# Attention in units of both heads, the causal mask added by TensorE, one maximum per unit, and a new written order up to MLP 1's ninth step

## The chip, the cores and the metric

The kernel runs on 1 core of one Trainium2 chip. The metric is the device time of one execution in microseconds (us). The engines are named as in the profile: PE is TensorE (PEld its weight loads), DVE VectorE, ACT ScalarE, POOL GpSimd, SP SyncE. Each engine works through its own instructions in the order in which the program writes them.

## The reference

The function computes causal attention with a learned decay, then two MLPs on its output. Cut to what matters:

```python
scores = scale * np.matmul(q, k.transpose(0, 1, 3, 2))        # 2 batches x 8 heads, 576 x 64
cum = np.cumsum(np.maximum(s, 0.0), axis=-1)
bias = -(cum[:, :, :, None] - cum[:, :, None, :])
scores = np.where(causal, -1000000000.0, scores + np.minimum(bias, 0.0))
scores = scores - np.max(scores, axis=-1, keepdims=True)
attn = np.exp(scores)
attn = attn / (np.sum(attn, axis=-1, keepdims=True) + 1e-09)
x = np.matmul(attn, v)                                        # -> 1152 tokens x 512
xn = x / np.sqrt(np.mean(x * x, axis=-1, keepdims=True) + 1e-06) * rms_g
h1 = (silu(xn @ w_gate) * (xn @ w_val)) @ w_out               # d_ff 1536
h = h1 @ w_in                                                 # d_ff 2048
out = (h * np.tanh(log1p(exp(h)))) @ w_out2
```

## The kernel before

**Attention.** The 16 heads go as 8 pairs of heads (NP). For a pair the scores are products of 64 rows of queries with 64 rows of keys, each split in a high and a low part so that one product of 128 rows (L359) and one of 68 rows (L360; four of these carry the bias of the decay) give them exactly enough. A head's 576 rows are tiles 0 to 3 of 128 rows and a last one of 64. `qk_unit` writes five units per pair: u0 and u1 hold tiles 0 and 1 of head 0 and head 1, in one PSUM bank each; u2 and u3 hold tiles 2 and 3 of head 0 and head 1, two banks each; u4 holds the last 64 rows of both heads, in two banks (L366, L367). Four single banks (`psS`) take them in turn. For each piece of a unit one custom VectorE instruction (`maxes`, L384) adds the causal mask from SBUF, multiplies by -0.125, writes the sum back and leaves the minimum in `sbias`; ScalarE takes the exponential with that bias and leaves the row's sum (`exps`, L391). TensorE transposes the probabilities (`pt_transposes`, L407), ScalarE, for u3 VectorE, copies them out (`pt_evac`), and TensorE multiplies with V in two parts (`av_op`, L445): part 0 for tiles 0 and 1, part 1 for the rest. The result is copied (`xt_evac`), transposed back (`x_transposes`, L456, tile xq) and multiplied by the reciprocal of the sums (`recips`, L462 to L465, and `x_norm`, L475).

For each pair POOL issues the transfers of keys and queries (`load_k`, `load_q`, `load_cum`), and computes three of the four low parts (`k_lo` L125, `q_lo` L131); VectorE computes the fourth. While attention runs, weights are already loaded and converted (`w_load`, `w_a` on ScalarE, `w_b` on VectorE at L276 and L278, `w_c` on ScalarE and, as long as attention runs, POOL at L296); `w_tick` does one such step.

**MLP 1.** Tokens go in blocks of 384. A step (b, f) multiplies block b by gate and value chunk f (`gate_val`, L549, 24 matmuls into two banks, gv), `silu_a` makes mbuf, `silu_b` splits it in the two parts of hhl, and `y_acc` (L583, 12 matmuls) adds the step to four banks. Batch 1's normalisation falls into the first steps: squares (`xn_sq`), twelve small VectorE operations for the reciprocal root (`rsqrt_ops`, L489 to L499), scaling, four times five transposes (`xn_mm`, L517) and the copies xh and xl (`xn_evac`, L523 and L524).

**What sets the order.** Everything is written out by hand: `at(t, f, ...)` collects calls with a time t in units, they are sorted by t and called in that order; attention uses this, and MLP 1's steps from k = 1 on are a loop behind it. No scheduler moves anything.

Of the kernel before, what the change touches and what calls it, by code (L numbers as in the profile page):

```python
# [12 lines left out]
ALU = mybir.AluOpType  # L13

# [29 lines left out]
def tile_kernel(ctx: ExitStack, tc: tile.TileContext, kq, qq, v, s, w1, w2, rms_g, out):  # L44
# [7 lines left out]
    psS = [ctx.enter_context(ExitStack())]  # L52
    psS.append(psS[0].enter_context(tc.tile_pool(name="psS", bufs=4, space=bass.MemoryType.PSUM)))
# [17 lines left out]
    raw = [[rawt[2 * i + h][:, 0:S] for h in range(2)] for i in range(2)]  # L71

# [4 lines left out]
    for i in range(2):  # L77
# [9 lines left out]
        PTB.append([w[:, 1280 * h:1280 * h + 1280].rearrange("p (c n) -> p c n", c=4) for h in range(2)])  # L87
        PTA.append([w[:, 2560:2944], xat[i][:, 2560:2944]])
        PTC.append([w[0:64, 2944 + 64 * h:3008 + 64 * h] for h in range(2)])
# [63 lines left out]
    nc.gpsimd.memset(mask16, 0.0)  # L153
    nc.gpsimd.affine_select(out=mask16[:, 384:512], in_=mask16[:, 384:512], pattern=[[-1, 128]], compare_op=ALU.is_ge,
                            fill=-8e9, base=0, channel_multiplier=1)
# [28 lines left out]
    def gates(h, x, pools):  # L184
        co = slice(64 + 288 * x, 352 + 288 * x)
        t = []
        for y, (pool, tag) in enumerate(pools):
            t.append(pool.tile([128, 512], F32, tag=tag, name="gates"))
# [6 lines left out]
    pT, pX, pS = (psT, "T"), (psX, "X"), (psS[1], "S")  # L195
# [12 lines left out]
    k_lo(0, 1, nc.gpsimd)  # L208
    nc.gpsimd.memset(mask16j, 0.0)
    for h in range(2):  # L210
        m = mask16j[64 * h:64 * h + 64, 224:288]
        nc.gpsimd.affine_select(out=m, in_=m, pattern=[[-1, 64]], compare_op=ALU.is_ge, fill=-8e9, base=0,
                                channel_multiplier=1)
# [112 lines left out]
    NU = 5 * NP  # L326


    def unit_tiles(u):
        return (0, 1) if u < 2 else (2, 3)  # L330

    s_tile = {}
    pos = [(2, 0, 1, 3, 4).index(i) if i < 5 else i for i in range(NU)]

    def s_views(i):
        u, t = i % 5, s_tile[i]
        if u == 4:
# [12 lines left out]
    def qk_unit(i):  # L350
        p, u = divmod(i, 5)
        z = p % 2
        s_tile[i] = [psS[1].tile([128, 512], F32, tag="S", name="sc") for _ in range(1 if u < 2 else 2)]
        if u < 4:
            hh = u % 2
            for o, n in zip(s_views(i), unit_tiles(u)):
                qs = slice(704 * hh + 128 * n, 704 * hh + 128 * n + 128)
                ks = slice(S * hh, S * hh + 128 * (n + 1))
                nc.tensor.matmul(o, QA[z][:, qs], KA[z][:, ks], start=(n != 1), stop=False)  # L359
                nc.tensor.matmul(o, QB[z][0:68, qs], KB[z][0:68, ks], start=False, stop=(n != 0))  # L360
        else:
            for n, o in enumerate(s_views(i)):
                for hh in range(2):
                    qs = slice(512 + 64 * hh, 640 + 64 * hh)
                    ks = slice(S * hh + 288 * n, S * hh + 288 * n + 288)
                    nc.tensor.matmul(o, QB[z][0:68, qs], KB[z][0:68, ks], start=(hh == 0), stop=False)  # L366
                    nc.tensor.matmul(o, QA[z][:, qs], KA[z][:, ks], start=False, stop=(hh == 1))  # L367

    def ring_col(i):
        return 2 * (pos[i] % 4)  # L370

    def sum_cols(i):

        p, u = divmod(i, 5)
        c = 12 * (p % 2)
        return [c + 8, c + 9] if u == 4 else [c + 2 * n + u % 2 for n in unit_tiles(u)]

    def maxes(i):

        for x, sv in enumerate(s_views(i)):  # L380
            u, c = i % 5, ring_col(i) + x
            m = (mask16[:, 0:288], mask16j)[x] if u == 4 else mask16[:, 512 - sv.shape[-1]:512]
            first = 3e38 if u < 4 or x == 0 else sbias[:, c - 1:c]
            nc.vector.tensor_tensor_reduce(out=sv, in0=sv, in1=m, scale=-0.125, scalar=first, op0=ALU.add, op1=ALU.min,  # L384
                                           accum_out=sbias[:, c:c + 1])

    def exps(i):
        c = ring_col(i)
        for x, (sv, pv, sc) in enumerate(zip(s_views(i), p_views(i), sum_cols(i))):
            x = 1 if i % 5 == 4 else x  # L390
            nc.scalar.activation(out=pv, in_=sv, func=ACTF.Exp, bias=sbias[:, c + x:c + x + 1], scale=-1.0,  # L391
# [9 lines left out]
    def pt_transposes(i):  # L401
        u = i % 5
        t_tile[i] = []
        for a, e, rows in pt_parts(u):
            t = psT.tile([128, 512], F32, tag="T", name="tp")
            for o in range(a, e, 128):
                nc.tensor.transpose(t[0:rows, o - a:o - a + 128], P[pos[i] % 2][:, o:min(e, o + 128)], ident)  # L407
            t_tile[i].append(t)

    def pt_evac(i):  # L410
        p, u = divmod(i, 5)
        z, t = p % 2, t_tile.pop(i)
        if u < 2:
            cp = [(PTA[z][u], t[0][:, 0:384])]
        elif u < 4:
            cp = [(PTB[z][u - 2][:, 0:n, 128 * y:128 * y + 128], t[y][:, 0:128 * n].rearrange("p (c n) -> p c n", c=n))
                  for y, n in enumerate((3, 4))]
        else:
            cp = [(PTB[z][h][:, :, 256:320], t[0].rearrange("p (c n) -> p c n", c=4)[:, :, 64 * h:64 * h + 64])
                  for h in range(2)]  # L420
            cp += [(PTC[z][h], t[1][0:64, 64 * h:64 * h + 64]) for h in range(2)]
        for dst, src in cp:
            if u == 3:
                nc.vector.tensor_copy(out=dst, in_=src)
            else:
                nc.scalar.copy(out=dst, in_=src)
# [3 lines left out]
    def av_op(p, part, c):  # L430
# [5 lines left out]
        for h in range(2):  # L436
# [463 lines left out]
```

## Time and profile before

| | us |
|---|---|
| median of 3 runs | 557.2 (555.62 to 557.57) |
| the profiled execution's own time | 557.82 |
| its span in the trace | 556.0 |
| PE busy | 535.5 (96%) |
| DVE busy | 284.8 (51%) |
| ACT busy | 255.8 (46%) |
| POOL busy | 66.8 (12%) |
| mean granted TensorE clock | 0.991 of full speed |

The span runs from the first to the last instruction of the trace; the execution's own time has 1.8 us around it. Busy time of one engine overlaps that of the others.

### The profile page before, as it was taken

The numbers are of one execution on the slowest core, as the hardware profiler recorded it, in microseconds if no ns is written. First come the engines' busy times: TensorE is split into PE (matmuls) and PEld (weight loads), VectorE is DVE, ScalarE is ACT, GpSimd is POOL, SyncE is SP. The second block draws the span as 40 slices with busy tenths as digits, with TensorE's granted clock in tenths as the row PEclk, the third lists the DMA queues.
The fourth block names the chain that finished last, engine by engine and source line by source line (L and its number), as shares of the span: only waits on it lengthen the run. The fifth ranks groups of instructions, "written<-read, shape, count | busy, mean of one in ns | idle before, by whom it ended". The sixth has DMA issues, their size and how long they took to land.

```text
span 556.0 us, 7854 instructions
## 1 busy us (share of the span) xinstructions
PE 535.5 (96%) x3008; PEld 484.5 (87%) x3008; DVE 284.8 (51%) x626; ACT 255.8 (46%) x581; POOL 66.8 (12%) x77
## 2 busy tenths in 40 slices
PE   5989999999699999999999999999999999999997
PEld 4666766789589999999999999999899899899895
DVE  7769999868736733677422256488711011011011
ACT  6767998858726522455321144455512211221211
POOL 6557856300000000000000000000000000000000
PEclk9989999999889999999999999999999999999999
DMA  9889894256714521554400004025201000010001
GB/s 239 224 228 230 241 239 121 77 192 228 223 39 146 159 75 34 168 177 152 151 2 1 0 4 144 6 78 184 79 0 58 1 0 1 0 58 1 1 0 58
DMA packets 18782, 55.91 MB, mean 101 GB/s; under 512 B 2348, under 2 KB 2604, under 8 KB 18716
## 3 DMA queue, kind: packets, MB, share of 16 engines
q1 hardware_dynamic: 13520, 42.04, 23.5%
q0 software_dynamic: 3712, 9.70, 8.5%
q10 hardware_dynamic: 1512, 3.66, 2.3%
q8 instruction: 24, 0.39, 0.3%
q14 instruction: 14, 0.11, 0.1%
HBM read 52.73 MB, written 2.66 MB: 100 GB/s over the span
## 4 chain that ended last, share of the span: by engine, by line
PE 84%; DVE 6%; DMA 3%; issue 2%; ACT 2%; POOL 1%; POOLq 0%; ACTq 0%; DVEq 0%
PE gv L549 25%; PE gv L618 18%; PE o L659 18%; PE y L583 12%; PE xa L445 4%; PE tp L407 3%; DMA w<-in_kq_dram 1%; DMA w<-in_qq_dram 1%; PE sc L360 1%; PE sc L359 1%; DVE sc L384 1%; PE xq L456 1%; DVE w L296 1%; DMA scr<-cC 1%; POOL w L131 1%
## 5 line engine op out<-in xcount | busy, mean ns | idle before, releaser
L549 PE MATMUL gv<-xh,wt 128*128 128x384 f32 x384 | 102.0, 336 | 1.2 <-DVE xl L524 1.2
L646 DVE TENSOR_TENSOR glb<-u,glb 128x768 fp32r<-128x768 f32 (+1 forms) x25 | 23.1, 925 | 115.8 <-ACT glb L645 115.7
L549 PEld LDWEIGHTS gv<-xh,wt 128*128 128x128 f32 x384 | 69.8, 188 | 1.5 <-issue 1.3
L557 ACT ACTIVATE mbuf<-gv 128x384 f32<-128x384 f32 x36 | 17.7, 493 | 107.0 <-PE gv L549 107.0
L659 PE MATMUL o<-wt,glb 128*128 128x512 f32 x270 | 66.9, 393 | 0.0
L558 DVE TENSOR_TENSOR mbuf<-mbuf,gv 128x384 f32<-128x384 f32 x36 | 19.9, 554 | 89.1 <-ACT mbuf L557 89.1
L549 PE MATMUL gv<-xl,wt 128*128 128x384 f32 x192 | 64.4, 335 | 0.0
L618 PE MATMUL gv<-xh,wt 128*128 128x384 f32 x240 | 63.7, 336 | 0.0
L659 PEld LDWEIGHTS o<-wt,glb 128*128 128x128 f32 x270 | 50.5, 188 | 10.6
L549 PE MATMUL gv<-xh,w 128*128 128x384 f32 x192 | 53.0, 348 | 2.7 <-DVE xl L524 2.7
L583 PE MATMUL y<-hhl,wt 128*128 128x384 f32 x288 | 53.6, 336 | 0.0
L583 PEld LDWEIGHTS y<-hhl,wt 128*128 128x128 f32 x288 | 50.4, 188 | 0.0
L391 ACT ACTIVATE px<-sc,cst 128x384 f32<-128x384 f32 (+2 forms) x80 | 41.4, 524 | 9.7 <-DVE cst L384 9.1
L636 ACT ACTIVATE u<-gv 128x768 f32<-128x768 f32 (+1 forms) x25 | 19.6, 788 | 54.9 <-PE gv L618 54.9
L645 ACT CAST glb<-u 128x768 fp32r<-128x768 f32 (+1 forms) x25 | 20.3, 814 | 53.1 <-PE o L659 49.9
L618 PEld LDWEIGHTS gv<-xh,wt 128*128 128x128 f32 x240 | 43.6, 188 | 0.5
L659 PE MATMUL o<-w,glb 128*128 128x512 f32 x162 | 41.1, 392 | 0.0
L618 PE MATMUL gv<-xl,wt 128*128 128x384 f32 x120 | 40.3, 336 | 0.0
L549 PEld LDWEIGHTS gv<-xh,w 128*128 128x128 f32 x192 | 36.7, 197 | 2.8 <-issue 2.8
L618 PE MATMUL gv<-xh,w 128*128 128x384 f32 x144 | 37.9, 335 | 0.0
L278 DVE SCALAR_TENSOR_TENSOR r<-r 128x512 int32<-128x512 int32 x47 | 35.4, 753 | 3.4 <-ACT r L268 1.7
L384 DVE CUSTOM_DVE_ANT_0 sc<-sc,xtm 128x384 f32<-128x384 f32 (+4 forms) x72 | 34.7, 503 | 2.9 <-PE sc L360 1.1
(138 smaller groups left out, 966.6 us busy)
## 6 DMA issues: line engine op xcount, KB each, us to landing
r<-in_w_dram SPq DMA_DIRECT2D x45, 512.0 KB, 3.4
stage_w<-in_w_dram SPq DMA_DIRECT2D x21, 512.0 KB, 4.7
w<-in_kq_dram POOLq DMA_DIRECT2D x7, 576.0 KB, 6.8
w<-in_qq_dram POOLq DMA_DIRECT2D x7, 576.0 KB, 7.4
out_dram<-osb SPq DMA_DIRECT2D x8, 256.0 KB, 3.2
px<-in_v_dram SPq DMA_DIRECT2D x5, 320.0 KB
r<-in_w_dram ACTq DMA_DIRECT2D x2, 512.0 KB, 5.8
px<-in_v_dram ACTq DMA_DIRECT2D x3, 320.0 KB
```

Source lines behind the costliest of these rows:

```text
L278: nc.vector.scalar_tensor_tensor(out=low, in0=top, scalar=3, in1=low, op0=ALU.logical_shift_left, op1=ALU.bitwise_or)
L384: nc.vector.tensor_tensor_reduce(out=sv, in0=sv, in1=m, scale=-0.125, scalar=first, op0=ALU.add, op1=ALU.min, accum_out=sbias[:, c:c + 1])
L391: nc.scalar.activation(out=pv, in_=sv, func=ACTF.Exp, bias=sbias[:, c + x:c + x + 1], scale=-1.0, accum_out=ssum[:, sc:sc + 1])
L445: nc.tensor.matmul(o, V[z][0:rows, c, ds], r, start=(c == 0), stop=(c == (1, 4)[part]))
L549: nc.tensor.matmul(t[:, g, 0:nt], wt[f][:, a, g, 128 * c:128 * c + 128], xhl[r][:, c, t0:t0 + nt], start=(n == 0), stop=(n == 11))
L558: nc.vector.tensor_tensor(out=tm, in0=tm, in1=t[:, 1, 0:nt], op=ALU.mult)
L583: nc.tensor.matmul(y_t[b][d], wt[f][:, a, 2, 128 * d:128 * d + 128], hhl[:, r, 0:BLK1[b][1]], start=((b, f) in FIRST and y == 0), stop=((b ...
L618: nc.tensor.matmul(t[:, x, 0:TB], w[:, a, 128 * c:128 * c + 128], xhl[r][:, c, TB * b:TB * b + TB], start=(n == 0), stop=(n == 11))
L636: nc.scalar.activation(out=u[:, xs], in_=h[:, xs, 0:TB], func=ACTF.Mish)
L645: nc.scalar.copy(out=gl[:, 0, xs], in_=u[:, xs])
L646: nc.vector.tensor_tensor(out=gl[:, 1, xs], in0=u[:, xs], in1=gl[:, 0, xs].bitcast(F32), op=ALU.subtract)
L659: nc.tensor.matmul(o_t[b][tt], gl[:, r, x, 128 * tt:128 * tt + 128], w[:, a], start=(g == 0 and x == 0 and y == 0), stop=(g == NG - 1 and ...
```

## The change

Attention now has four units per pair, each with both heads and one tile of two banks: u0 tiles 0 and 1 (bank n holds tile n of both heads), u1 tile 2, u2 tile 3 (a bank per head), u3 the last 64 rows of both heads, 576 columns wide. `psS` has two such tiles and stays for MLP 1. The mask is added by TensorE, as a product of a bf16 identity with a bf16 mask at the end of each bank's chain: seven a pair, with a weight load each. The maxima are plain reductions of whole units (two for u0, one for the others) and one multiplication by -0.125 in `sbias` per unit. Exponentials are nine a pair, with a scale of 0.125. VectorE copies out both tiles of u1's and of u3's transposes, ScalarE the rest. The four products of part 0 with V stand together. Head 1's first `k_lo` goes from POOL to VectorE, and the mask's building is other. The times of all calls come from a new table T, and MLP 1's steps 1 to 8 are collected in the same list with times of their own.

```diff
+    psS = ctx.enter_context(tc.tile_pool(name="psS", bufs=2, space=bass.MemoryType.PSUM))
...
-    k_lo(0, 1, nc.gpsimd)
...
+    k_lo(0, 1)
...
-    NU = 5 * NP
+    NU = 4 * NP
...
+        s_tile[i] = t = psS.tile([128, 2, 512], F32, tag="S", name="sc")
...
+        if u == 0:
+            for n in range(2):
+                w = 128 * (n + 1)
+                for hh in range(2):
+                    tile_of(n, hh, n, t[:, n, w * hh:w * hh + w])
+                o = t[:, n, 0:2 * w].rearrange("p (h k) -> p h k", h=2)[:, :, 128 * n:w]
+                todo[n].append((o, ident16, mask16.unsqueeze(1).to_broadcast([128, 2, 128])))
+        elif u < 3:
+            w = 128 * (u + 2)
+            for hh in range(2):
+                tile_of(u + 1, hh, hh, t[:, hh, 0:w])
+                todo[hh].append((t[:, hh, w - 128:w], ident16, mask16))
...
+            todo[1].append((t[:, 1, 224:288], ident16, mask16j))
+        for x in todo:
+            for n, (o, q, k) in enumerate(x):
+                nc.tensor.matmul(o, q, k, start=(n == 0), stop=(n == len(x) - 1))
...
-            nc.vector.tensor_tensor_reduce(out=sv, in0=sv, in1=m, scale=-0.125, scalar=first, op0=ALU.add, op1=ALU.min,
-                                           accum_out=sbias[:, c:c + 1])
...
+                nc.vector.tensor_reduce(out=sbias[:, c + 2 * n:c + 2 * n + 2], op=ALU.max, axis=AX.X,
+                                        in_=t[:, n, 0:2 * w].rearrange("p (h k) -> p h k", h=2))
+        elif u < 3:
+            nc.vector.tensor_reduce(out=sbias[:, c:c + 2], in_=t[:, :, 0:128 * (u + 2)], op=ALU.max, axis=AX.X)
+        else:
+            nc.vector.tensor_reduce(out=sbias[:, c:c + 1], in_=t[:, :, 0:288], op=ALU.max, axis=AX.XY)
+        b = sbias[:, c:c + (4, 2, 2, 1)[u]]
+        nc.vector.tensor_scalar(out=b, in0=b, scalar1=-0.125, scalar2=None, op0=ALU.mult)
...
-            nc.scalar.activation(out=pv, in_=sv, func=ACTF.Exp, bias=sbias[:, c + x:c + x + 1], scale=-1.0,
+            nc.scalar.activation(out=pv, in_=sv, func=ACTF.Exp, bias=sbias[:, c + x:c + x + 1], scale=0.125,
...
+        "max": (0.4, 0.85, 0.84, 0.36), "exp": (0.9, 1.66, 1.7, 1.0),
+        "pt": ((1.65, 1.75), (1.93, 1.85), (1.9, 1.97), (2.29, 1.95)),
...
+    K0 = 9
+    at(60 + T["sb"][0], silu_b, 0, 0)
+    for k in range(1, K0):
```

The order of the transposes, on PE in the middle of attention. Names: sc are scores, tp transposed probabilities, px the probabilities, w_71 the tile of keys and queries. Before, where the last row of tp is u0's, the first four rows are the scores of u1 and the four with 384 and 512 columns those of u2:

```order
L359 MATMUL sc<-w_71 128x128
L360 MATMUL sc<-w_71 128x128
L359 MATMUL sc<-w_71 128x256
L360 MATMUL sc<-w_71 128x256
L407 MATMUL tp<-cst,px 128x128 x4
L407 MATMUL tp<-cst,px 64x128
L359 MATMUL sc<-w_71 128x384
L360 MATMUL sc<-w_71 128x384
L359 MATMUL sc<-w_71 128x512
L360 MATMUL sc<-w_71 128x512
L407 MATMUL tp<-cst,px 128x128 x3
```

Two units' scores stand between u0's transposes and u0's own scores, which are a few rows further up in the same form as u1's; and five transposes of the pair before.

The same place of the change on PE; u0's eight products with its two masks stand right ahead of the first row, and u0's transposes begin with the row of one tile from xtm:

```order
L425 MATMUL tp<-cst,px 64x128
L373 MATMUL sc<-w_71 128x384 x2
L373 LDWEIGHTS px
L373 MATMUL sc<-px 128x128
L373 MATMUL sc<-w_71 128x384 x2
L373 LDWEIGHTS px
L373 MATMUL sc<-px 128x128
L425 MATMUL tp<-cst,px 128x128 x4
L472 MATMUL xq<-cst,xtm 128x128 x2
L425 MATMUL tp<-cst,xtm 128x128
L425 MATMUL tp<-cst,px 128x128 x2
```

Between u0's scores and u0's transposes stand one unit's scores, five transposes of the pair before and xq.

DVE at the start of MLP 1, steps 2 and 3 of before (mbuf and hhl are the steps' outputs; L276, L278 and L296 are a conversion's three parts; the twelve operations of the reciprocal root begin at L489):

```order
L558 TENSOR_TENSOR mbuf<-mbuf,gv 128x384
L276 TENSOR_SCALAR stage_w_1457<-stage_w_1457 128x512
L278 SCALAR_TENSOR_TENSOR stage_w_1457<-stage_w_1457 128x512
L296 TENSOR_TENSOR w_71<-stage_w_1457,w_71 128x512
L565 TENSOR_TENSOR hhl<-mbuf,hhl 128x384
L489 TENSOR_SCALAR cst<-cst 128x5
L491 TENSOR_SCALAR cst<-cst 128x5
```

and the same place of the change, from the last three of the twelve on:

```order
L510 TENSOR_TENSOR cst<-cst 128x5
L511 SCALAR_TENSOR_TENSOR cst<-cst 128x5
L513 SCALAR_TENSOR_TENSOR cst<-cst 128x5
L574 TENSOR_TENSOR hhl<-mbuf,hhl 128x384
L284 TENSOR_SCALAR r_1445<-r_1445 128x512
L286 SCALAR_TENSOR_TENSOR r_1445<-r_1445 128x512
L304 TENSOR_TENSOR w_71<-r_1443,w_71 128x512
```

The twelve operations stood behind hhl of step 2 and now stand ahead of it; between hhl of step 1 and mbuf of step 2 there are four conversions where there were two.

DVE at step 4 of MLP 1, before:

```order
L558 TENSOR_TENSOR mbuf<-mbuf,gv 128x384
L276 TENSOR_SCALAR stage_w_1457<-stage_w_1457 128x512
L278 SCALAR_TENSOR_TENSOR stage_w_1457<-stage_w_1457 128x512
L296 TENSOR_TENSOR w_71<-stage_w_1457,w_71 128x512
L565 TENSOR_TENSOR hhl<-mbuf,hhl 128x384
L524 SCALAR_TENSOR_TENSOR xl<-gv,cst,xh 128x512
L524 SCALAR_TENSOR_TENSOR xl<-gv,cst,xh 128x64
```

and in the change:

```order
L567 TENSOR_TENSOR mbuf<-mbuf,gv 128x384
L538 SCALAR_TENSOR_TENSOR xl<-gv,cst,xh 128x512
L538 SCALAR_TENSOR_TENSOR xl<-gv,cst,xh 128x64
L574 TENSOR_TENSOR hhl<-mbuf,hhl 128x384
L284 TENSOR_SCALAR stage_w_1437<-stage_w_1437 128x512
L286 SCALAR_TENSOR_TENSOR stage_w_1437<-stage_w_1437 128x512
L304 TENSOR_TENSOR w_71<-stage_w_1437,w_71 128x512
```

The two rows of xl, which read out the banks of the first chunk's transposes, moved from behind the conversion and hhl to directly behind mbuf.

## Rows read from the trace of the kernel before

**Rows 1.** The page: busy time of the engines, and a group's mean ns.

```profile
PE 535.5 (96%) x3008; PEld 484.5 (87%) x3008; DVE 284.8 (51%) x626; ACT 255.8 (46%) x581; POOL 66.8 (12%) x77
...
L278 DVE SCALAR_TENSOR_TENSOR r<-r 128x512 int32<-128x512 int32 x47 | 35.4, 753 | 3.4 <-ACT r L268 1.7
```

**Rows 2.** Stretches: us; busy PE, PEld, DVE, ACT, POOL; clock; DMA; GB/s.

```profile
43.38:54.70 11.32, 11.32 (x86) 8.06 (x82) 10.87 (x30) 9.60 (x32) 7.77 (x8) 1.00 0.95 223
...
33.50:109.95 76.45, 75.07 (x522) 52.88 (x523) 70.84 (x213) 64.58 (x214) 47.95 (x45) 0.98 0.73 189
...
109.95:162.53 52.58, 46.48 (x256) 42.86 (x255) 36.64 (x82) 34.08 (x70) 0.00 (x0) 0.94 0.54 174
...
150.60:157.60 7.00, 7.00 (x25) 6.97 (x26) 1.04 (x2) 0.42 (x2) 0.00 (x0) 0.57 0.18 66
```

**Rows 3.** Waits (us, times, longest), and the chain that ended last, MLP 1.

```profile
PE gv L549 <- DVE xl L524: 3.9, 2, 2.7
...
PE gv L517 <- DVE mbuf L558: 1.4, 1, 1.4
...
150.59 7.16 PE gv L549 x24
...
169.04 4.16 PE gv L549 x24
173.20 2.08 PE y L583 x12
```

**Rows 4.** Timeline of PE in pair 3: start, us, instruction.

```profile
48.19 0.28 PE L360 MATMUL sc<-w 68*128 68x128 f32 x1
48.30 0.33 PE L359 MATMUL sc<-w 128*128 128x256 f32 x1
...
50.38 0.76 PE L445 MATMUL xa<-aw,px 128*64 128x320 f32 x4
```

**Rows 5.** Timeline: a product, its maximum, and an exponential of 256 columns.

```profile
41.68 0.34 PE L360 MATMUL sc<-w 68*128 68x384 f32 x1
...
42.17 0.57 DVE L384 CUSTOM_DVE_ANT_0 sc<-sc,xtm 128x384 f32<-128x384 f32 x1 [0.54 <-PE sc L360]
...
50.58 0.47 ACT L391 ACTIVATE px<-sc,cst 128x256 f32<-128x256 f32 x1
```

**Rows 6.** Groups of DVE by form, 43.38 to 54.70: busy us, mean ns, idle.

```profile
L131 DVE TENSOR_TENSOR w<-raw_r,w 64x576 fp32r<-64x576 f32 x1 | 1.8, 1821 | 0.0
L278 DVE SCALAR_TENSOR_TENSOR r<-r 128x512 int32<-128x512 int32 x1 | 1.7, 1741 | 0.0
L384 DVE CUSTOM_DVE_ANT_0 sc<-sc,xtm 128x512 f32<-128x512 f32 x2 | 1.5, 731 | 0.0
```

**Rows 7.** Timeline of DVE and POOL; then L463's durations: ns min/median/max.

```profile
49.73 1.30 POOL L296 TENSOR_TENSOR wt<-r,wt 128x512 fp32r<-128x512 f32 x1 [1.85 <-issue]
...
49.89 1.17 DVE L463 TENSOR_SCALAR cst<-cst 128x9 f32<-128x9 f32 x1
...
L463 DVE TENSOR_SCALAR cst<-cst x8: 173/664/1250, 23.8 to 112.2; 128x9 f32<-128x9 f32 x8
```

**Rows 8.** Timeline: pair 0's first long product, head 1's q_lo, pair 2's first product.

```profile
8.69 0.69 PE L359 MATMUL sc<-w 128*128 128x384 f32 x1
...
10.52 0.75 DVE L131 TENSOR_TENSOR w<-raw_hB,w 64x576 fp32r<-64x576 f32 x1 [1.77 <-DMA w<-in_qq_dram]
...
33.50 0.33 PE L360 MATMUL sc<-w 68*128 68x128 f32 x1 [1.56 <-POOL w L131]
```

**Rows 9.** Timeline of DVE behind hhl of step 2, and y of step 2.

```profile
133.77 0.17 DVE L489 TENSOR_SCALAR cst<-cst 128x5 f32<-128x5 f32 x1
...
135.53 2.25 PE L583 MATMUL y<-hhl,wt 128*128 128x384 f32 x12
...
136.13 0.42 DVE L276 TENSOR_SCALAR r<-r 128x512 int32<-128x512 int32 x1
...
137.80 0.42 DVE L276 TENSOR_SCALAR r<-r 128x512 int32<-128x512 int32 x1
```

More of the change, by code (lines that the diff above doesn't have):

```diff
@@ L13 @@
 ALU = mybir.AluOpType
+AX = mybir.AxisListType
 B, H, S, D = 2, 8, 576, 64
@@ L152, in tile_kernel @@
     load_k(1)
[L153 to L155 removed]
+    nc.gpsimd.memset(m16[:, 0:320], 0.0)
+    nc.gpsimd.affine_select(out=ident16, in_=ident16, pattern=[[-1, 128]], compare_op=ALU.not_equal,
+                            fill=1.0, base=0, channel_multiplier=1)
+    nc.gpsimd.affine_select(out=mask16, in_=mask16, pattern=[[-1, 128]], compare_op=ALU.is_ge, fill=-8e9, base=0,
+                            channel_multiplier=1)
+    for h in range(2):
+        m = mask16j[64 * h:64 * h + 64]
+        nc.gpsimd.affine_select(out=m, in_=m, pattern=[[-1, 64]], compare_op=ALU.is_ge, fill=-8e9, base=0,
+                                channel_multiplier=1)
     load_q(1)
@@ L350, in qk_unit @@
     def qk_unit(i):
-        p, u = divmod(i, 5)
+        p, u = divmod(i, 4)
         z = p % 2
[L353 to L360, printed above, removed]
+        s_tile[i] = t = psS.tile([128, 2, 512], F32, tag="S", name="sc")
@@ L361, in qk_unit @@
         else:
-            for n, o in enumerate(s_views(i)):
+            for n in range(2):
                 for hh in range(2):
@@ L399, in tile_kernel, with pt_parts @@
-    t_tile = {}
[L401 to L417, printed above, removed]
-        else:
[L419 to L426, printed above, removed]
+    def pt_parts(i):
+        u, w = i % 4, P[(i + 1) % 2]
+        if u == 0:
+            return [[w[1][:, 128 * h:128 * h + 128], w[0][:, 256 * h:256 * h + 128], w[0][:, 256 * h + 128:256 * h + 256]]
+                    for h in range(2)]
+        if u < 3:
+            return [[w[h][:, 128 * c:128 * c + 128] for c in range(u + 2)] for h in range(2)]
+        return [[px[:, 128 * c:128 * c + 128] for c in range(4)], [px[:, 512:576]]]
@@ new lines, in tile_kernel, with pt_transposes, pt_evac @@
+    t_tile = {}
+    def pt_transposes(i, y):
+        t = psT.tile([128, 512], F32, tag="T", name="tp")
+        for c, x in enumerate(pt_parts(i)[y]):
+            nc.tensor.transpose(t[0:x.shape[-1], 128 * c:128 * c + 128], x, ident)
+        t_tile[i, y] = t
+    def pt_evac(i, y, eng):
+        p, u = divmod(i, 4)
+        z, t = p % 2, t_tile.pop((i, y))
+        if u == 0:
+            dst, src = PTA[z][y], t[:, 0:384]
+        elif u < 3:
+            n = u + 2
+            dst, src = (PTB[z][:, 0:n, y, 128 * (u - 1):128 * u], t[:, 0:128 * n].rearrange("p (c n) -> p c n", c=n))
+        elif y == 0:
+            dst, src = PTB[z][:, :, :, 256:320], t.rearrange("p (c h n) -> p c h n", c=4, h=2)
+        else:
+            dst, src = PTC[z], t[0:64, 0:128]
+        if eng is nc.vector:
+            nc.vector.tensor_copy(out=dst, in_=src)
+        else:
+            nc.scalar.copy(out=dst, in_=src)
@@ L525, in xn_evac @@
                                            op1=ALU.subtract)
-    def banksT():
-        return [psT.tile([128, 512], F32, tag="T", name="bank") for _ in range(2)]
-    def banksS():
-        return psS[1].tile([128, 2, 512], F32, tag="S", name="gv")
     xhl = [sbt([128, KD, NTOK], F32R, n, n) for n in ("xh", "xl")]
```

246 lines of the change are left out of this document (120 added, 126 removed), and 9 rows, old and new, of the table T.

## Prediction

> **What bounds the kernel now.** The page first: TensorE is busy for 96% of the span, VectorE and ScalarE for about half [rows 1]. So it is TensorE's work and its few gaps that count. The table of stretches then splits the part that the change touches. One pair of the middle of attention takes 11.32 us, and TensorE is busy in all of it; VectorE is busy for 10.87 of the same 11.32, so it is nearly as full, and POOL for 7.77 [rows 2]. Attention from the first matmul of pair 2 to MLP 1's first matmul takes 76.45 us, MLP 1's start from there to its seventh product gv 52.58 [rows 2]. In that start the waits and the chain show what is not work: TensorE waited 3.9 us twice for VectorE's xl and 1.4 us for its mbuf, and behind the longer wait 24 matmuls took 7.16 us which take 4.16 a little later [rows 3]. The granted clock of that stretch is 0.57 [rows 2], mostly the lower level of 1.2 GHz, and it costs 3.0 us. Behind that start gv (4.16) and y (2.08) follow each other without a gap [rows 3]; the change leaves that part alone, so it is costed at nothing.
>
> **Masks on TensorE, per pair.** Added: 7 matmuls with 64 to 256 columns and a weight load each. The nearest row is the short product with 68 rows and 128 columns: the next matmul starts 0.11 us behind it [rows 4]. 7 x 0.11 = +0.8 us. Bounds: 0.4, if loads and columns slide under the neighbours better than there, and 1.4 at twice the row, if the change of operand type breaks the pipelining. I take the row, which is of the same shape. The Trainium skill ("TensorE: Matmul & The Clock Gate", Back-to-back issue gap) gives about 81 ns for a sustained matmul of 128 columns; by it the term would be an estimated 0.6. The row here is longer, and the sum goes by the row.
>
> **One run fewer.** The first half of V's products of a pair now stands in one place and not in two. Four such matmuls in a run of their own take 0.76 us [rows 4]; at the pair's mean of 11.32 / 86 = 0.13 us they would be 0.53. The rest is the run's own end: -0.2 us a pair (bounds 0 and -0.4).
>
> **A new wait.** In before, the transposes of u0 stand behind two further units and seven and five other transposes (the first order rows show the last part). Now u0's probabilities are transposed when only one unit, five transposes of u3 and xq have gone by (the second order rows): 1 + 6 + 4 + 2 = 13 instructions, at 0.13 each about 1.75 us. In that time must pass: from the last matmul to VectorE's start (41.68 + 0.34 to 42.17: 0.15 us) [rows 5]; the maximum of the 512 wide bank, 0.73 [rows 6]; the new multiplication by -0.125, 0.17 where nothing holds it [rows 7]; three exponentials at up to 0.47 [rows 5], one behind the other 1.2 in all; and two more hand-overs, to ScalarE and back to TensorE, taken at 0.15 too. Together 2.6. TensorE waits about 0.9 us in each pair. Bounds: 0.3, and 1.9 if the multiplication is held once (below). The period is 11.32 + 0.8 - 0.2 + 0.9 = 12.8 us.
>
> **Is VectorE still in time?** Of the 10.87 us [rows 2], three operations were held: L131 1.82 against 0.75 elsewhere [rows 6, 8], L278 1.74 against its mean of 0.75 [rows 1, 6], and L463 1.17 against 0.17 [rows 7], 3.1 us in all. So the bare work is 7.8. The maxima now go through 3136 columns at 0.73 per 512, 4.5, and four multiplications at 0.2, 0.8; before, ten pieces with their read-outs were about 4.9: +0.4. Two more copies out of PSUM, +0.8, and a shorter reciprocal part, -0.2. Bare 8.8, with the same holds 11.9 of 12.8: just in time. ScalarE loses one exponential and some copies a pair and isn't near its limit.
>
> **Attention in sum.** Six pairs' worth at 12.8 = 76.8, and the transposes of the normalised x, 20 matmuls at 0.13 = 2.6, of which one set (0.6) falls into a wait: 78.8 against 76.45, **+2.35 us**. (Before's 76.45 holds the same 20 and its own waits and slow clock, which I let go with the old order.)
>
> **The start.** The first unit of before needs one head, and its first long product started at 8.69 us; the new u0 needs both, and head 1's low part ends at 10.52 + 0.75 = 11.27 [rows 8]. From there two pairs at 12.8, less 1.0 in all for the products that the first has nothing to do for, give 35.9 for pair 2, against 33.50: **+2.4 us**. Bounds: 0, since before stood 1.56 us for POOL in front of pair 2 [rows 8], which an earlier arrival of the same data would now hide; and +4.1, a third of a period more, if the first pair's units wait for each other as the later ones do. The masks' building on POOL, one more fill and one more selection, lies ahead of the first unit's data and costs nothing; head 1's low part of the keys goes from POOL to VectorE, 0.75 [rows 8], which the wait for the queries' part hides (without that cover it is 0.75).
>
> **MLP 1's start.** TensorE's order stays as it was; VectorE's and ScalarE's changes. The work in the 52.58 us at full clock: six gv at 4.16 and five y at 2.08 [rows 3], 35.4; the other 52 of its 256 instructions [rows 2], transposes and attention's last products, at 0.13, 6.8; in sum 42.2, so 10.4 is lost. Of that 3.9 + 1.4 are the waits and 3.0 the clock [rows 3], 2.1 the rest. In the new order xl of the first chunk stands right behind mbuf of step 4 (the last order rows), ahead of a conversion and hhl, so the banks come free some 2 us sooner and the waits for xl and mbuf should go, the slow clock with them; of the rest I let half stay, 1.0. Against that, the twelve small operations of the reciprocal root and one more conversion now stand ahead of hhl of step 2: 136.13 - 133.77 = 2.36 and 137.80 - 136.13 = 1.67 [rows 9], 4.0 later. It was ready at about 133.8 and y of step 2 began at 135.53 [rows 9], so 1.7 is slack; y would wait 2.3, or nothing if other waits of VectorE shrink. I take 1.8. 42.2 + 1.0 + 1.8 = 45.0: **-7.6 us**. SP's and POOL's transfers keep their order in this part; the weights' loads follow the conversions, whose number ahead of step 4 is the same.
>
> **Sum.** +2.35 + 2.4 - 7.6 = -2.85 on the profiled 557.8: 554.95. The median shown is 0.6 below the profiled run, so 554.4 us, -0.5%. A measurement of this kernel tells about 0.5% (2.8 us) from no change.
>
> **Rivals.** *A, the new wait isn't there.* If masks cost 0.4, and the exponentials are ready with 0.3 us of wait, the period is 11.32 + 0.4 - 0.2 + 0.3 = 11.8 and attention 73.4 with the transposes, not 78.8: 554.4 - 5.4, about **549 us**. For it speaks that pairs of before ran without a gap; against it the sum of rows 5 to 7. *B, MLP 1's gain is half taken back.* If the wait of y in step 2 lowers the clock as the wait of 2.7 did (7.16 for 4.16) [rows 3], 3.0 us stay: -4.6 in place of -7.6, **557.4 us**, no change. For it speaks that just such a wait is planned there; against it that it is shorter. *C, the other side: POOL holds VectorE.* A TENSOR_SCALAR of 128x9 took 0.17 us alone and 1.17 when POOL's subtraction ran (49.73 to 51.03) [rows 7]; over eight pairs its median is 0.66 [rows 7]. The change puts four more of that kind into each pair, on the way from scores to exponentials. POOL is busy 7.77 us in a pair [rows 2]. If three of four are held for 1.0, VectorE needs 11.9 + 2.6 = 14.5 us, 1.7 above the period: 6 x 1.4 to 1.7, about +8 with a part hidden: **562 us**. It decides from about 0.9 us of new holds a pair on, where VectorE passes 12.8. Against it: POOL's subtractions start when data land, and in the new order the first two units' maxima fall largely ahead of that. The Trainium skill ("SBUF — State Buffer", Who interferes with whom) says that VectorE and GpSimd share one port pair under an exclusive lock, that tensor_scalar can take it and tensor_reduce never does. By that rule the maxima themselves are never held and the multiplications are. The trace agrees for the multiplication: 1.17 against 0.17.
>
> **How the numbers follow.** Forecast 0.45 (its own range 551 to 558), A 0.14, B 0.17, C 0.24. A gives the lower end, 547 with a better start, C the upper, 562.5. Faster by over 0.5%: 0.27 of the forecast, A and a little of B, 0.42. Within 0.5%: 0.16 of the forecast, 0.15 of B and 0.01 of C, 0.32. Slower: most of C and the forecast's and B's ends, 0.26.
>
> **What would show it.** Right: a period near 12.8 with one wait of TensorE of about 0.9 for u0's exponentials, seven mask matmuls at some 0.11, pair 2 near 36 us, no long wait for xl and mbuf, one short wait for hhl in step 2. Wrong: a period under 12 (A), granted clock near half behind y's wait (B), the new multiplication with a median of 0.6 or more and TensorE waiting for VectorE in every unit (C).

## The result and the profile after

The changed kernel takes 560.27 us (median of 5 runs, 559.6 to 562.42) against 557.2: 1.0065 of the time before, 95% interval 1.004 to 1.009. It is slower by 0.65%; I had forecast 554.4, faster by 0.5%.

The profiled execution took 562.42 us with a span of 560.6. TensorE's clock was low in it for one stretch in pair 6, which a second profile of the same program doesn't show (span 557.6, the fifth experiment); both are used below.

Stretches of the changed kernel. The columns are those of [rows 2]. The first is a pair in the middle of attention, the next two are pairs 6 and 7, then come all of attention from pair 2's first product to MLP 1's first, and MLP 1's start up to its seventh gv:

```profile
59.13:72.15 13.02, 12.23 (x93) 8.32 (x91) 10.48 (x22) 8.55 (x27) 7.68 (x8) 1.00 0.82 205
...
85.18:103.24 18.06, 16.10 (x97) 9.97 (x96) 13.78 (x36) 10.23 (x31) 12.43 (x13) 0.81 0.61 149
103.24:117.27 14.03, 12.88 (x97) 8.91 (x96) 11.70 (x23) 9.66 (x28) 4.64 (x5) 1.00 0.28 95
36.39:122.34 85.95, 79.62 (x558) 53.32 (x556) 69.39 (x155) 58.78 (x176) 45.52 (x44) 0.96 0.65 168
122.34:167.08 44.74, 42.97 (x255) 40.04 (x255) 35.96 (x78) 33.18 (x66) 0.00 (x0) 1.00 0.63 212
```

Against [rows 2]: MLP 1's start went from 52.58 us to 44.74, attention from 76.45 to 85.95, and pair 2 began at 36.39 in place of 33.50 [rows 8]. That is -7.8 + 9.5 + 2.9 = +4.6, the difference of the two spans (560.6 - 556.0). So the gain of MLP 1 came, and attention took it and more. Behind MLP 1's start nothing changed.

The same stretches in the second profile, at full clock:

```profile
85.02:100.17 15.15, 13.19 (x97) 8.73 (x96) 13.10 (x36) 10.40 (x31) 9.76 (x11) 1.00 0.74 182
100.17:114.20 14.03, 12.88 (x97) 8.90 (x96) 11.70 (x23) 9.52 (x28) 7.96 (x8) 1.00 0.29 92
36.51:119.27 82.76, 76.49 (x558) 51.96 (x556) 68.70 (x155) 58.87 (x176) 45.53 (x44) 1.00 0.71 174
119.27:164.01 44.74, 42.97 (x255) 40.04 (x254) 35.92 (x78) 33.17 (x66) 0.00 (x0) 1.00 0.66 212
```

Attention is at 82.76 here, +6.3, and pair 6 at 15.15 in place of 18.06. The low clock cost the first profile some 3 us. The loss doesn't hang on it: of the 15 executions of the changed kernel (these five and the ten of the fifth experiment) the eleven with a mean granted clock of 0.999 or 1.000, called full clock below, lie at 559.0 to 560.5 us with a median of 559.7, the four with 0.993 to 0.997 at 560.6 to 563.2.

Where a middle pair's 13.02 us goes is seen in its timelines (first profile; start, length, instruction, and in brackets the idle time ahead of it and what ended it). TensorE, from u0's last mask to u0's transposes:

```profile
50.78 0.28 PE L373 MATMUL sc<-px 128*128 128x256 bf16 x1
50.90 0.27 PE L425 MATMUL tp<-cst,px 128*64 128x128 f32 x1
...
52.36 0.38 PE L472 MATMUL xq<-cst,xtm 128*128 128x128 f32 x2
53.25 0.30 PE L425 MATMUL tp<-cst,xtm 128*128 128x128 f32 x1 [0.51 <-DVE aw L441]
53.83 0.44 PE L425 MATMUL tp<-cst,px 128*128 128x128 f32 x2 [0.28 <-ACT px L407]
```

VectorE and ScalarE in the same time:

```profile
51.17 1.02 DVE L395 TENSOR_REDUCE cst<-sc 128x2 f32<-128x256 f32 x2 [1.21 <-PE tp L425]
52.23 0.17 DVE L402 TENSOR_SCALAR cst<-cst 128x4 f32<-128x4 f32 x1
...
52.83 0.87 DVE L441 COPY aw<-tp 64x128 f32<-64x128 f32 x2
...
52.51 0.37 ACT L407 ACTIVATE xtm<-sc,cst 128x128 f32<-128x128 f32 x1 [1.25 <-DVE cst L477]
52.87 0.36 ACT L407 ACTIVATE xtm<-sc,cst 128x128 f32<-128x128 f32 x1
53.21 0.47 ACT L407 ACTIVATE px<-sc,cst 128x256 f32<-128x256 f32 x1
```

The chain is the predicted one: u0's scores end at 51.06, the maxima start at 51.17, the third exponential ends at 53.68, TensorE goes on at 53.83. That is 2.8 us; I had 2.6, with the maximum of the 512 wide bank alone (0.73), where both of u0's maxima lie in the chain, 1.02 in sum. VectorE stood idle for 1.21 us ahead of them; why the first bank's maximum didn't start under the second bank's scores is not shown. The work of TensorE under the chain is shorter than I had: the thirteen instructions that I counted begin at 50.90, and xq begins at 52.36 and its two transposes take 0.11 each from start to start, so TensorE could go on at 52.58. That is 0.13 an instruction, as I took it. But they begin 0.16 us ahead of the scores' modelled end, from which the chain is counted, so they cover 1.5 us of it, not 1.75. The idle time in brackets (0.51 + 0.28) is less than the loss, since the modelled ends of the pipelined instructions reach into it. From start to start the loss is 53.25 - 52.58 and 53.83 - 53.36, 0.67 + 0.47 = 1.14; u0's other transposes, which follow one by one behind the exponentials, lose the rest of what the next table shows.

A sum over all starts in a steady pair (before: 43.38 to 66.09; after: 46.11 to 85.18; each instruction counted to the start of the next, worked out from the trace) gives the whole difference of the period:

| us per pair | before | after |
|---|---|---|
| scores | 4.27 | 4.24 |
| 7 mask products | 0 | 0.61 |
| products with V | 3.64 | 3.46 |
| transposes tp and xq | 3.45 | 4.72 |
| period | 11.36 | 13.02 |

+0.61 for the masks, -0.18 for the run that fell away, +1.27 for the transposes, whose number is the same: that is the wait, in the places where it falls.

### The profile page after: what moved, and what is told of

Same layout as the page of the kernel before. It is cut to its first block, busy times and chain, and to the rows that moved or that the text cites. A ratio compares the mean times of both kernels' runs of the same rounds, so it can differ in the third digit from the quotient of the medians.

```text
span 560.6 us, 7821 instructions
## 1 busy us (share of the span) xinstructions
PE 539.1 (96%) x3064; PEld 483.5 (86%) x3064; DVE 284.8 (51%) x547; ACT 248.9 (44%) x533; POOL 64.6 (12%) x76
## 4 chain that ended last, share of the span: by engine, by line
PE 89%; DVE 5%; DMA 2%; ACT 2%; issue 1%; POOL 0%; SPq 0%; ACTq 0%; DVEq 0%; POOLq 0%
PE gv L558 24%; PE gv L629 18%; PE o L671 18%; PE y L593 13%; PE sc L373 6%; PE xa L462 5%; PE tp L425 4%; DMA w<-in_qq_dram 1%; DMA r<-in_w_dram 1%; ACT xtm L407 1%; DVE cst L395 1%; DVE w L304 1%; PE xq L472 1%; ACT px L407 0%; PE gv L531 0%
## 5 line engine op out<-in xcount | busy, mean ns | idle before, releaser
L558 PE MATMUL gv<-xh,w 128*128 128x384 f32 x192 | 51.0, 336 | 0.0
L373 PE MATMUL sc<-w 128*128 128x288 f32 (+4 forms) x192 | 44.1, 360 | 2.1 <-DMA w<-in_qq_dram 0.9
L629 PE MATMUL gv<-xh,w 128*128 128x384 f32 x144 | 37.9, 335 | 0.0
L558 PEld LDWEIGHTS gv<-xl,wt 128*128 128x128 f32 x192 | 36.1, 188 | 0.1
L286 DVE SCALAR_TENSOR_TENSOR r<-r 128x512 int32<-128x512 int32 x47 | 33.7, 717 | 4.1 <-ACT r L276 1.7
L671 PEld LDWEIGHTS o<-w,glb 128*128 128x128 f32 x162 | 30.3, 188 | 6.0
```

Of the source, the lines that this page charges most:

```text
L286: nc.vector.scalar_tensor_tensor(out=low, in0=top, scalar=3, in1=low, op0=ALU.logical_shift_left, op1=ALU.bitwise_or)
L373: nc.tensor.matmul(o, q, k, start=(n == 0), stop=(n == len(x) - 1))
L558: nc.tensor.matmul(t[:, g, 0:nt], wt[f][:, a, g, 128 * c:128 * c + 128], xhl[r][:, c, t0:t0 + nt], start=(n == 0), stop=(n == 11))
L629: nc.tensor.matmul(t[:, x, 0:TB], w[:, a, 128 * c:128 * c + 128], xhl[r][:, c, TB * b:TB * b + TB], start=(n == 0), stop=(n == 11))
L671: nc.tensor.matmul(o_t[b][tt], gl[:, r, x, 128 * tt:128 * tt + 128], w[:, a], start=(g == 0 and x == 0 and y == 0), stop=(g == NG - 1 and ...
```

## Experiments

All times of before in these runs lie at 557.05 to 557.81 us (medians). MLP 1's first gv, the end of attention, is named with each; it stood at 109.95 before and at 122.34 and 119.27 in the two profiles of the changed kernel.

**1. Only MLP 1's new order, with the attention of before.** The events of MLP 1's steps 1 to 8 and their times are put into the kernel before:

```diff
-    for k in range(1, len(steps1) - 1):
+    K0 = 9
+    at(60 + T["sb"][0], silu_b, 0, 0)
+    for k in range(1, K0):
...
+    for k in range(K0, len(steps1) - 1):
```

> The kernel before with its own attention, and only MLP 1's steps 1 to 8 in the new written order. Theory (the new order of MLP 1's start is worth what the walk gave, and attention in the new units loses more than that): MLP 1's start falls from 52.6 us to about 45, the time to about 549.5 us, 1.4% below before. Rival (the short start in the changed kernel needs its own attention, because more conversions are done by then or because buffers come free sooner): the gain is under 3 us, 554 to 557.

Measured: 550.59 us, 0.9895 of before (0.987 to 0.992). Its profile:

```profile
34.81:110.51 75.70, 74.17 (x526) 51.80 (x523) 71.81 (x213) 64.55 (x215) 45.74 (x43) 1.00 0.75 195
110.51:155.45 44.94, 43.41 (x255) 40.10 (x254) 36.00 (x81) 33.24 (x68) 0.00 (x0) 1.00 0.66 211
```

The theory holds. MLP 1's start takes 44.94 us behind the old attention too, against 44.74 in the changed kernel. This version beats both kernels, by 1.05% and, in medians, by 1.7%.

**2. Without eight of the twelve operations of batch 0's reciprocal root.** (Part of the computation is left out.)

```diff
-    at(T["nops"], lambda: nops.extend(rsqrt_ops()))
+    at(T["nops"], lambda: nops.extend(rsqrt_ops()[:4]))
```

> The changed kernel without the last eight of the twelve small VectorE operations of batch 0's reciprocal root (a part of the computation is left out; the rest is unchanged). Theory (in pair 6 these eight stand in front of the copies that TensorE waits for, so its two waits there of 1.18 and 0.78 us are theirs, and TensorE's clock falls behind them): pair 6's period falls from 18.1 us to 13 to 14, the time by 2 to 4 us against the changed kernel, to about 557. Rival (TensorE's low clock behind pair 6 has to do with the normalised columns or with POOL): the period stays at 16 to 18, the time within 1 us of the changed kernel.

Measured: 559.67 us; pair 6 takes 15.13 us at full clock, first gv at 119.00. That is more than the 13 to 14 of the theory, and the time didn't fall to 557. Against the first profile pair 6 gained 2.9 us, but against the second (15.15 with all twelve operations) nothing: the two waits in pair 6 shrink from 1.18 and 0.78 us to the usual 0.51 and 0.28, and in their place TensorE waits 0.95 us for the copy xl a little later in the same pair:

```profile
99.60 0.55 PE L425 MATMUL tp<-cst,px 128*128 128x128 f32 x3 [0.95 <-DVE xl L538]
```

The wait moved. One part of the theory is borne out: all six executions have full clock, where the changed kernel has it in 11 of 15.

**3. Without the masks.** (The causal mask is left out.)

```diff
-                todo[n].append((o, ident16, mask16.unsqueeze(1).to_broadcast([128, 2, 128])))
...
-                todo[hh].append((t[:, hh, w - 128:w], ident16, mask16))
...
-            todo[1].append((t[:, 1, 224:288], ident16, mask16j))
```

> The changed kernel without the 56 mask products on TensorE (the causal mask is left out, all else is unchanged). Theory (a mask product costs 0.08 to 0.11 us of TensorE's time and part of it comes back as a longer wait for u0's exponentials): the period of a pair falls from 13.0 to 12.5, the time by 3 to 4 us, to about 556.5. Rival (VectorE and ScalarE hold the period): the period stays above 12.9 and the time within 1 us of the changed kernel. If the masks were the whole loss of attention, it would fall by some 9 us to 551.

Measured: 557.99 us, 1.0027 of before (1.001 to 1.005), 2.3 below the changed kernel's first median, with a period of 12.55 us:

```profile
45.50:58.05 12.55, 11.59 (x85) 8.13 (x84) 10.50 (x22) 8.55 (x27) 7.68 (x8) 1.00 0.86 222
```

The period is that of the theory; the time fell by less than its 3 to 4 us, but seven of the twelve executions had a low clock, and the five at full clock have a median of 556.5, 3.2 below the changed kernel's 559.7. The masks cost 0.48 of the 1.66 us, less than their 0.61 on TensorE: the two transposes xq with the wait behind them and xq's other three take 1.54 us a pair in place of 1.37, since u0's chain still has to pass while TensorE has less to do. In this profile too the clock was low in pair 6 (17.57 us).

**4. u2's transposes behind the next u0's scores.**

```diff
-        "pt": ((1.65, 1.75), (1.93, 1.85), (1.9, 1.97), (2.29, 1.95)),
+        "pt": ((1.65, 1.75), (1.93, 1.85), (2.05, 2.06), (2.29, 1.95)),
```

> The changed kernel with u2's eight transposes written behind u0's scores of the next pair, not ahead of them, so that TensorE has 0.85 us more to do before u0's transposes. Theory (TensorE waits about 1.1 us a pair between xq and u0's transposes, for the chain from u0's scores to its exponentials): the wait falls to about 0.3, the period from 13.0 to about 12.3, the time by 5 to 6 us to about 554.5. Rival (the wait's end is set by VectorE's copies of u3 or by VectorE's load, which do not move): the period stays at 12.9 to 13.1, the time within 1 us of the changed kernel.

Measured: 559.29 us, first gv at 120.13; the period falls by 0.36 us, not 0.7, and the first pairs give it back (pair 2's last unit starts 2.0 us later than in the second profile). In a middle pair:

```profile
66.37 0.39 ACT L466 COPY xtm<-xa 128x256 f32<-128x256 f32 x1
66.63 0.39 ACT L407 ACTIVATE xtm<-sc,cst 128x128 f32<-128x128 f32 x1
...
67.98 0.44 PE L425 MATMUL tp<-cst,px 128*128 128x128 f32 x2 [0.39 <-ACT px L407]
```

The exponential now begins right behind ScalarE's copies, those of u2, which came later with u2's transposes, and the one shown, while the multiplication was done at 66.27. ScalarE's queue has become the end of the wait. Neither text has it: the wait shrinks, and the next engine on the chain holds half of it.

**5. The changed kernel again.**

> The changed kernel once more, unaltered. Four of its five first times (559.6 to 560.6 us) are some 2 us below that of the profiled run (562.4), whose clock was low in pair 6. Theory (the low clock is not in every run, and the attention of the new units is slow without it): a profile at full clock shows a period of 13.0 us, pair 6 at 15 to 16 and not 18.1, MLP 1's first matmul near 120. Rival (the low clock is part of the change's price): pair 6 near 18 again.

Measured: 559.84 us, 1.0045 of before (1.002 to 1.007); the profile is shown above. The theory holds: pair 6 at 15.15, first gv at 119.27.

**6. The reciprocals behind the copies of u3.**

```diff
-        "xn": (6.19, 8.37), "rec": 4.63, "wa": 4.0, "wb0": 6.29, "wb1": 6.8, "wc": 8.96,
+        "xn": (6.19, 8.37), "rec": 5.84, "wa": 4.0, "wb0": 6.29, "wb1": 6.8, "wc": 8.96,
```

> The changed kernel with the reciprocals' three VectorE operations behind the two copies of u3, not ahead of them: the copy that the profile names as the end of TensorE's longest wait (0.51 us a pair) comes 0.5 us sooner. Theory (the wait belongs to the chain from u0's scores over maximum and exponentials, and the copy ends only its first half): the second half grows by what the first loses, the period stays at 13.0, the time within 1 us of the changed kernel. Rival (the copy is the cause): the period falls by about 0.5 to 12.5, the time by 3 to 4 us.

Measured: 559.32 us, period 13.03:

```profile
52.36 0.38 PE L472 MATMUL xq<-cst,xtm 128*128 128x128 f32 x2
53.03 0.33 PE L425 MATMUL tp<-cst,xtm 128*128 128x128 f32 x1 [0.29 <-ACT xtm L407]
53.83 0.44 PE L425 MATMUL tp<-cst,px 128*128 128x128 f32 x2 [0.48 <-ACT px L407]
```

The first transpose starts 0.22 us sooner and the second at the same 53.83. The copy that the view names as the releaser of the longer wait is not what the pair waits for. Neither text has the end of attention: pair 6 takes 14.70 us and pair 7 13.39, 1.1 less in sum, and the stretch behind them gives 0.6 of it back (5.67 for 5.06). All ten executions have full clock.

**7. Without the multiplication.** (The exponentials' biases are not scaled.)

```diff
-        b = sbias[:, c:c + (4, 2, 2, 1)[u]]
-        nc.vector.tensor_scalar(out=b, in0=b, scalar1=-0.125, scalar2=None, op0=ALU.mult)
```

> The changed kernel without the 32 multiplications by -0.125 (the exponentials get wrong biases; all else is unchanged). Theory (the chain from u0's scores to its exponentials ends the wait): it is shorter by the multiplication's 0.17 and its hand-over, the period falls by 0.2 to 0.3 us to about 12.8, the time by 1.5 to 2.5 us. Rival 1 (POOL holds the multiplications, as I gave a chance of one in four): the period falls by 0.8 or more. Rival 2 (the wait has another end): no change.

Measured: period 12.80 to 12.81, 0.22 less, first gv at 118.38. The time, 559.13 us (557.35 to 562.32), is scattered with the clock, which was low in five of the ten executions; the five at full clock have a median of 557.9, 1.8 below the changed kernel's 559.7. The theory holds and POOL's hold as the price of the multiplication does not.

**8. The squares and the root earlier.**

```diff
-        "sq": (19.09, 19.21, 22.96, 22.71, 21.91), "nops": 23.17, "xs": (25.93, 28.01, 30.67, 32.14),
+        "sq": (19.09, 19.21, 22.35, 22.25, 21.91), "nops": 22.4, "xs": (25.93, 28.01, 30.67, 32.14),
...
-        for _ in range(2):
+        for _ in range(3):
```

> The changed kernel with batch 0's squares and reciprocal root written earlier, so that none of the twelve small VectorE operations stands between u0's maxima and the copies of u3 in pair 6. Theory (as in the run without the last eight of them): pair 6 at about 15.1 us at full clock, the time 559.2 to 559.8, 0.5 to 1 us below the changed kernel. Rival (six operations now ahead of u2's maxima of pair 5 cost as much there): no gain, 560 to 561.

Measured: 563.71 us, 1.0109 of before: worse than either text. VectorE, POOL and TensorE in pair 6:

```profile
84.77 0.83 DVE L503 TENSOR_SCALAR cst<-cst 128x5 f32<-128x5 f32 x1 [0.89 <-ACT w L498]
85.64 1.34 DVE L505 TENSOR_SCALAR cst<-cst 128x5 int32<-128x5 int32 x1
87.01 0.17 DVE L507 TENSOR_SCALAR cst<-cst 128x5 int32<-128x5 int32 x1
87.22 1.26 DVE L510 TENSOR_TENSOR cst<-cst 128x5 f32<-128x5 f32 x1
...
84.17 1.41 POOL L132 TENSOR_TENSOR w<-raw_hA,w 64x576 fp32r<-64x576 f32 x1
85.54 1.41 POOL L132 TENSOR_TENSOR w<-raw_hB,w 64x576 fp32r<-64x576 f32 x1
87.02 1.43 POOL L138 TENSOR_TENSOR w<-raw_hA,w 64x576 fp32r<-64x576 f32 x1
...
91.74 0.66 PE L425 MATMUL tp<-cst,px 128*128 128x128 f32 x4 [2.40 <-DVE aw L441]
```

Operations of five columns, 0.17 us elsewhere, take 0.83, 1.34 and 1.26 and end with POOL's subtractions. They stand ahead of u2's maxima, so TensorE waits 2.40 us, and its clock is low behind that. The pair takes 18.80 us, 3.65 more than at full clock in the changed kernel. Another 1.5 us of this profile are lost early, between the last units of pairs 1 and 2 (14.50 for 13.02), where TensorE waits 1.26 us for a low part that POOL computes; the edit doesn't touch that place. Here rival C's mechanism is at work, but not at the place that I gave it.

**9. Without POOL's scaling of batch 0.** (The four columns are not scaled.)

```diff
-        at(T["xs"][c], xn_scale, 0, c)
```

> The changed kernel without POOL's scaling of batch 0's columns (4 pairs of products on POOL are left out; all else is unchanged). Theory (in pairs 6 and 7 POOL is busy without a pause, and it holds VectorE's conversion and u2's multiplication, 1.5, 1.3 and 1.1 us where they take 0.4, 0.7 and 0.2 alone, so the copies xl that free TensorE's banks come late): pair 6 falls from 15.15 us to 14 to 14.5, MLP 1's first matmul from 119.3 to 118 to 118.5, the time by 1 us. Rival (the copies xl are late because of their place behind u0's and u2's maxima, not because of POOL): pair 6 within 0.3 us of 15.15.

Measured: 561.16 us (559.59 to 563.24); pair 6 takes 15.16, the two waits are 1.18 and 0.78 as before. The three executions at full clock lie at 559.6 to 560.1, as the changed kernel does. The theory fell: POOL's scaling isn't what makes pair 6 long.

**10. u0's maxima over 8 columns of each head.** (Part of the maximum is left out.)

```diff
-                                        in_=t[:, n, 0:2 * w].rearrange("p (h k) -> p h k", h=2))
+                                        in_=t[:, n, 0:2 * w].rearrange("p (h k) -> p h k", h=2)[:, :, 0:8])
```

> The changed kernel with u0's two maxima taken over 8 columns of each head in place of 128 and 256 (a part of the maximum is left out, its place and waits stay). Theory (each pair's wait of 1.27 us on TensorE is the chain from u0's scores over maxima, multiplication and exponentials): the chain is shorter by some 0.6 to 0.7 us, the period falls from 13.03 to 12.3 to 12.5, the time by 4 to 5 us to about 555.5. Rival (another end of the wait, ScalarE's copies or VectorE's copies of u3, comes right behind): the period falls by 0.3 us at most, the time by under 2 us.

Measured: 554.86 us, 0.9948 of before (0.993 to 0.997):

```profile
57.00:69.25 12.25, 12.04 (x92) 8.31 (x91) 10.76 (x23) 8.82 (x27) 7.78 (x8) 1.00 0.90 219
```

The two maxima now take 0.25 us in place of 1.02. The period falls by those 0.77 us, the time by 5.0. With a chain that is only so much shorter, the changed kernel would have come out at my forecast. VectorE's own load isn't the reason: it is busy for 10.76 of 12.25 us here and for 10.48 of 13.02 in the changed kernel.

**11. The first two normalised columns behind the last unit's scores.**

```diff
-        "xm": (26.41, 28.4, 31.2, 32.77), "xe": (26.88, 28.76, 31.84, 32.8), "lim11": 29.72, "mlp": 32.84,
+        "xm": (31.02, 31.84, 32.5, 32.77), "xe": (31.25, 32.1, 32.6, 32.8), "lim11": 29.72, "mlp": 32.84,
```

> The changed kernel with the transposes of batch 0's first two normalised columns and their copies xh and xl written behind the last unit's scores, not in pairs 6 and 7. Theory (of the 2.1 us by which pair 6 is longer than the others, some 1.2 are the two waits behind the reciprocal root's operations and 0.8 the five transposes; of pair 7's 1.0 the transposes are 0.75 and the wait for xl is mostly given back): pair 6 falls to 14.2, pair 7 to 13.0, the tail grows by 1.5 to 3 us, the time stays within 1.5 us of the changed kernel. Rival (the banks that the two columns hold make the units of pairs 6 and 7 late): both fall to 13.0 to 13.3 and the time falls by 2 us or more.

Measured: 565.2 us; pair 6 takes 14.07 and pair 7 13.02, as the theory has it, but the tail grows from 5.1 to 11.7 us (expected 1.5 to 3 more): TensorE waits 2.95 us in one piece for the copy xl there:

```profile
119.15 0.92 PE L425 MATMUL tp<-cst,px 128*128 128x128 f32 x4 [2.95 <-DVE xl L538]
```

What the columns cost in the pairs is their work and 0.3 us of waits in each; pair 6's other 1.05 us stay with its two waits. In the tail they cost more than in the pairs, and the clock was low behind the long wait there.

## Why the prediction was wrong

**MLP 1's start: right, and to the size.** Predicted -7.6 us, measured -7.84 and, alone, -7.64. The wait for hhl in step 2 is there, 1.18 us where I took 1.8:

```profile
149.25 2.18 PE L593 MATMUL y<-hhl,wt 128*128 128x384 f32 x11 [1.18 <-DVE hhl L574]
```

The waits for xl and mbuf and the low clock are gone, as predicted. The clock didn't fall behind hhl's wait (rival B). Y's wait is 0.6 shorter than in the sum, and what stays beside it above the 42.2 of work is 1.4 and not 1.0; the total is as near as it is because the two offset each other. (The wait for xl that the prediction calls 3.9 us "twice" is 3.9 in sum, two waits; its sum took it so.)

**The start: right, a little small.** +2.4 predicted, 36.39 and 36.51 against 33.50 measured, +2.9 to +3.0. Where the 0.6 comes from stays open. (The upper bound, +4.1, doesn't follow from its words: a third of a period of 12.8 is 4.3, on top of the 2.4. Nothing hangs on it.)

**Attention in sum: the step that failed.** Predicted 78.8 us, measured 82.76 at full clock and 85.95 in the first profile. Two terms of that step were mis-sized: the new wait, and what the normalisation of batch 0 adds to pairs 6 and 7, whose waits I had put at nothing.

The period was 12.8 by the sum and 13.02 in the trace. Its parts were not right one by one: masks 0.61 and not 0.8, the run -0.18 and not -0.2, the wait 1.27 and not 0.9. Of the wait, 0.2 is a longer chain (both maxima are in it) and 0.25 a shorter cover: 13 instructions at 0.13 are 1.7, not 1.75, which the trace bears out, and 0.16 of that lies ahead of the point from which I counted the chain. Six pairs make +1.3. That the wait is this chain is shown by the seventh and the tenth run: what is taken off the chain comes off the period, 0.22 and 0.77 us. That it isn't the copy named in the view is shown by the sixth.

The larger one is the normalisation of batch 0. I took its 20 transposes at 0.13, let one set fall into a wait, and wrote 2.0; above six even periods (82.76 - 6 x 13.02) the second profile has 4.6. The five transposes of a column take 0.75 to 0.8 us, not 0.65, so four take 3.1. The rest, some 1.5, is waits: u0's chain and the copies of u3 lie behind the root's small operations in pair 6 (1.18 and 0.78 in place of 0.51 and 0.28), and in pair 7 TensorE waits 0.91 us for the copy xl:

```profile
92.83 0.30 PE L425 MATMUL tp<-cst,xtm 128*128 128x128 f32 x1 [1.18 <-ACT px L407]
94.13 0.33 PE L425 MATMUL tp<-cst,xtm 128*128 128x128 f32 x1 [0.78 <-DVE aw L441]
97.65 0.86 PE L531 MATMUL bank<-cst,w 128*128 128x128 f32 x5
107.81 0.66 PE L425 MATMUL tp<-cst,px 128*128 128x128 f32 x4 [0.91 <-DVE xl L538]
```

I had written that before's own waits there go with the old order. I had no row for that, and the trace of before spoke against it: its 76.45 is 8.3 above six pairs of 11.36, of which the 20 transposes are only 2.6. In the changed kernel waits stand in other places: without the root's operations 0.95 us appear at xl in the same pair, and with the columns moved away pair 6 is 14.07.

Together these are +0.6 for the start, +1.3 for the period, +2.6 for the normalisation and -0.2 for MLP 1: 4.3 us above the predicted sum. From profile to profile that is all: 557.8 - 2.85 + 4.3 = 559.3, and the second profile's execution took 559.34. The medians, 559.8 and 560.3, lie 1.1 to 1.6 above 554.4 + 4.3 = 558.7, because I took 0.6 off for before's median, while the changed kernel's medians lie 0.5 to 0.9 above that profiled execution, with the executions of a low clock in them. That clock goes with the first of the two waits in pair 6. Where a profile has it at 0.98 to 1.35 us (the changed kernel, its repetition, the third, seventh and ninth run) the mean clock was 0.992 to 0.997 in 19 of 43 executions; where it is 0.41 to 0.66 (the second, fourth, sixth and tenth) it was at least 0.998 in all 27; with 2.40 us, in the eighth, it was 0.994 to 0.996 in all five. (The eleventh, with 1.18, isn't counted, for its clock falls in the tail.) What brings the clock down in one execution and not in another of the same program is left open.

**Is VectorE in time?** Yes: 10.48 of 13.02 us, where I had 11.9 of 12.8. I let three old holds stay, and one of them is left: the conversion's first part takes 1.48 us where it takes 0.42 alone, but the reciprocal's addition, on whose 1.17 rival C rests, takes 0.15 to 0.17 in every pair now. The median of the 32 multiplications is 0.17 us; one of them takes over 0.3 in the first profile, four in the second (rival C, by its own mechanism, was wrong here). The forecast's own range, 551 to 558, missed the time. The outer end of the whole held it, and C's number was near, for another reason: that is luck.

**Rival A** is refuted by the same rows: the masks are cheap, but the wait is on the path in every pair.

The masks' price was nearer to the page's figure that I cited than to the row that I went by: 0.61 us in seven products, 0.087 each. The Trainium skill ("TensorE: Matmul & The Clock Gate", Back-to-back issue gap) has about 81 ns for 128 columns. The trace agrees in the mean: the four mask products of that width in the pair from 46.11 to 59.13 take 0.078 from start to start, single ones 0.04 to 0.16.

## What to carry to other kernels

Making units larger takes work off the engines and puts a longer unbroken chain (scores, maximum, scale, exponentials) in front of the next engine; count what stands in the waiting engine's queue under that chain, from the same moment as the chain, before counting busy time. A change of two parts should be costed and run as two: here the second alone is worth 6.5 us, and the first takes all of it and 3 us more. A releaser that a view names for a wait need not be the cause; take it away and see whether the next start moves.

## What the hardware showed that I hadn't expected

Operations of VectorE over five columns took 0.83, 1.34 and 1.26 us beside POOL's subtractions, against 0.17 undisturbed, and three of them set back a whole pair; the 32 multiplications of four columns or fewer had a median of 0.17 and a longest of 0.92 and 1.39 in the two profiles. A hold can also cost nothing: in the tenth run u1's multiplication is held for 1.31 us in three middle pairs, and the period is still the 0.77 us shorter. By the Trainium skill ("SBUF — State Buffer", Who interferes with whom) VectorE and GpSimd share a port pair under a lock; the trace agrees. In the eighth run's rows the price is the other engine's remaining time, however small the operation: the three end at 85.60, 86.98 and 88.48, POOL's subtractions at 85.58, 86.95 and 88.45.

Two reductions of u0, 1.02 us together on an engine that is idle for a fifth of the pair, were worth 0.77 us of TensorE's time when they were cut short, for they stand alone on the way from its scores to its transposes.
